# Order of evacuations in stage D, the form of stage A for one batch, and the place of one fold part, in an FFT and channel-mix kernel

## The chip, the cores and the metric

The kernel runs on one core of a Trainium2 chip. The metric is the device time of one execution in microseconds. TensorE multiplies matrices into PSUM, ScalarE and VectorE empty PSUM and compute elementwise, GpSimd and SyncE start DMAs. Each engine has its own instruction stream in program order; semaphores tie them together.

## The reference

```python
X = np.fft.fft(x, axis=1)            # x: 8 x 3072 x 256
X = np.fft.fft(X, axis=2)
x = X.real                           # input of the channel mix
x_prev = x shifted by one place along the sequence
xk = mu_k * x + (1 - mu_k) * x_prev
xr = mu_r * x + (1 - mu_r) * x_prev
k = np.maximum(xk @ w_k, 0.0)        # 256 -> 1024
v = k * k @ w_v                      # 1024 -> 256
r = 1.0 / (1.0 + np.exp(-(xr @ w_r)))
out = r * v                          # 8 x 3072 x 256, float32
```

## The kernel before, in words

The eight batches are computed one after the other, but in a software pipeline: while the channel mix of one batch runs, the Fourier transform of the next is made in between.

**Fourier transform of a batch.** *Fold* (VectorE): the sequence is added to its mirror image, in two parts h = 0 and 1. *quarters_1*, *quarters_2* (from batch 3 on; *butterfly* before that) make sums and differences over the feature axis on VectorE; quarters_2 is three instructions (L198, L200, L202) that write the tile eo. *Stage A* (TensorE): small matmuls of eo with tables, over the first factor of the sequence. *Stage D*: matmuls of stage A's result a with tables over the features, into g_all. *Stage C*: matmuls of g_all with the tables of the second factor, into pq. *halves*, *diff*, *mix* (VectorE) make the mixed inputs x of the channel mix.

**Channel mix.** The work is cut into 48 chunks of 512 places (8 batches, two mirror halves m, three parts each) and every chunk into four steps, so step 4n + ds is part ds of chunk n. In a step:

- a *k piece* (k_piece; matmuls L893, four of 512 columns) goes into a PSUM slot, and ScalarE's relu (L903) empties it; on every second step VectorE squares two pieces (L913);
- for each chunk an *r item* (L920, sigmoid L925), and the transform's items that are due ("x" items, added with at);
- a *v tile* (v_tile; L934, eight matmuls of 256 columns) of an earlier chunk, into half a bank, and after every second v tile an *output step* v_out: one VectorE instruction (L956) that multiplies and empties the bank, and two DMAs on SyncE's queue (L964);
- an *event*: a stage of the transform that works in two row groups of TensorE, rows 0 to 63 and 64 to 127 (matmuls L611 or L784). The steps listed in v_behind take their v tile out of the step and put it right behind the event before;
- the VectorE items that are due ("w" items). In the steps of OUT_FIRST the output step comes ahead of them, in others behind.

All of this order is written by hand as step numbers, and pin_order keeps it on every engine.

**PSUM.** Its eight banks are three double-bank slots, psW, handed out in turn by ps_w (k pieces, r items and the transform's stages take the next in the same ring), and two single banks, psV, handed out in turn by ps_v for the v tiles. v_bank gives a stage the psV bank that the next pair of v tiles will use: the *shared bank*. A slot or bank is written again only when everything that reads it is done. evac (L572, L574) is the evacuation; with "A" it is a ScalarE ACTIVATE.

**Stage A, two forms.** a_slot_0 computes slot 0 of the second part (two matmuls over 112 rows, L617) at an early step, with a small evacuation. a_all then computes all the rest in one event: three psW slots and the shared bank, pairs of matmuls of the two row groups side by side, and six evacuations of different sizes. For batch 2 these stand at steps 22 and 31.

**Stage D (d_all).** One event for the whole batch, at step s + 33 with s = 24t - 48, for batches t = 3 to 7: three psW slots and the shared bank; an evacuation of a slot is two ScalarE instructions. Behind it comes the v tile of step s + 34, then the k piece of s + 34 (into slot 0), the v tile of s + 35 (into the shared bank), the k pieces of s + 35 and s + 36 (slots 1 and 2), then an r item (slot 0 again).

**Around stage C of batch 2 (c_all, step 39).** It uses three slots and the shared bank, which the output step of step 38 empties. VectorE's order is: quarters_1 of batch 3 (step 36), quarters_2 (37), square (37), output step (38), fold of the second part (39), square (39).

Of the kernel before, what the change touches and what calls it, by code (L numbers as in the profile page):

```python
# [20 lines left out]
def _v(ap, extra_offset, free_dims):  # L21
    new_ap = [list(ap.ap[0])] + [[s, c] for (s, c) in free_dims]
    return dataclasses.replace(ap, offset=ap.offset + extra_offset, ap=new_ap)
# [16 lines left out]
def kernel(  # L40
# [10 lines left out]
    nc = tc.nc  # L51

    B, S, D = x.shape
    F = moe_w_k.shape[1]
    P = 128
    N1, R = 48, 64
    NSL = 27
    NU = 26
# [14 lines left out]
    def ps_slot(kind, n, cols):  # L73
        k = ps_n[kind] % n
        ps_n[kind] += 1
        return psum.tile([P, cols], FP32, name=f"ps{kind}{k}", tag=f"ps{kind}{k}", bufs=1)

    def ps_w():
        return ps_slot("W", 3, 1024)

    def ps_v():
        return ps_slot("V", 2, 512)
# [22 lines left out]
    xp_t, xm_t, p_t, eo_t = {}, {}, {}, {}  # L105
# [283 lines left out]
    w_h, w_h0 = w_hh[:, 0:WB], w_hh[:, WB:2 * WB]  # L389
# [176 lines left out]
    a_t = {}  # L566
# [3 lines left out]
    def evac(out_ap, in_ap, eng):  # L570
        if eng == "V":
            V.tensor_copy(out=out_ap, in_=in_ap)  # L572
        else:
            nc.scalar.activation(out=out_ap, in_=in_ap, func=AF.Copy)  # L574

    def a_tile(b):
        a_t[b] = y_pool.tile([P, 2, NU, 64], FP16, name="a")
# [23 lines left out]
    def v_bank():  # L601
        k = ps_n["V"] % 2
        return psum.tile([P, 512], FP32, name=f"psV{k}", tag=f"psV{k}", bufs=1)

    def side_by_side(lo, hi, n, f):
        for k in range(max(len(lo), len(hi))):
            if k == n:
                f()
            for items in (lo, hi):
                for out, w, r in items[k:k + 1]:  # L610
                    nc.tensor.matmul(out=out, lhsT=w, rhs=r, start=True, stop=True)  # L611
# [9 lines left out]
    def a_all(b):  # L621
# [13 lines left out]
        def out(ps, o, e, q, n, gs=(0, 1), step=512):  # L635
            evac(_v(a_t[b], 64 * NU * e + 16 * gs[0] + q, [(16, len(gs)), (32, WB), (1, n)]),
                 _v(ps, o, [(step, len(gs)), (1, WB), (WB, n)]), "A")
# [9 lines left out]
        out(ws[2], 0, 0, 9, 6)  # L647
        out(ws[2], 6 * WB, 1, 9, 3)

    def a_sum(b, h, i0, eng="A", m=4):  # L650


        if (h, i0) == (0, 0):
            a_tile(b)
        ps = ps_w() if m == 4 else ps_v()
        for i in range(m):
            parts = [(h, i0 + i + 1 - h, 0, 2 * WA, 0, 1)]
            if h and i0 + i == 7:
                parts = [(0, 0, 0, WA, WA, 1), (1, 7, 1, WA, 1, 2)]
            for half, q, o, n, w, step in parts:  # L660
                for k in range(2):
                    nc.tensor.matmul(out=_v(ps, 256 * i + o, [(2 * WA // n, n)]),  # L662
                                     lhsT=p_t[b, half][0:96, q, 128 * k:128 * k + 128],
                                     rhs=_v(w_pm[0:96], (WA + WB) * k + w,
                                            [(WA + WB, 2), (step, n // 2)]),
                                     start=(k == 0), stop=(k == 1))
        a_ps[b, h, i0] = ps
        if eng:
            a_evac(b, h, i0, eng, m)

    a_ps = {}

    def a_evac(b, h, i0, eng, m=4):
        evac(_v(a_t[b], 8 * h + i0, [(16, 2 * WA), (1, m)]),
             _v(a_ps[b, h, i0], 0, [(1, 2 * WA), (256, m)]), eng)
# [23 lines left out]
    def d_all(b):  # L699
        ws = [ps_w() for _ in range(3)]  # L700
        v = v_bank()

        def run(g, n):
            rows = (lo64, hi64)[g]
            ps, o, step = (ws[n], 512 * g, 256) if n < 3 else (v, 128 * g, 64)
            return [(ps[:, o + step * e + 64 * i:o + step * e + 64 * i + 64],
                     a_t[b][rows, e, 2 * u:2 * u + 2, :], w_d[rows, e])
                    for i, u in enumerate(range(4 * n, min(4 * n + 4, NU // 2))) for e in range(2)]

        def out(ps, n, k, gs=(0, 1), o=0, e=256):  # L710
            g, m = gs[0], len(gs)
            evac(_v(g_all, 1024 * n + g, [(1, m), (128, 2 * k), (2, 32)]),
                 _v(ps, o, [(512, m), (32, 2 * k), (1, 32)]), "A")
            evac(_v(g_all, 1024 * n + 64 + 128 * g, [(128, m), (256, k), (1, 64)]),
                 _v(ps, o + e, [(512, m), (64, k), (1, 64)]), "A")

        side_by_side(run(0, 3) + run(0, 0) + run(0, 1) + run(0, 2),
                     run(1, 0) + run(1, 1) + run(1, 2) + run(1, 3),
                     2, lambda: out(v, 3, 1, (0,), 0, 64))
        out(ws[0], 0, 4)  # L720
        out(ws[1], 1, 4)
        out(v, 3, 1, (1,), 128, 64)
        out(ws[2], 2, 4)

    def d_small(b, u, n, eng="A"):
# [214 lines left out]
    def v_part(c, ds, tbs):  # L940
        for tb in tbs:
            h = tb % 2
            if ds == 0 and h == 0:
                st["v", tb] = ps_v()
            for fc in (2 * ds, 2 * ds + 1):
                nc.tensor.matmul(out=st["v", tb - h][:, 256 * h:256 * h + 256],  # L946
                                 lhsT=k2_t[c][:, fc, 128 * tb:128 * tb + 128], rhs=wv_sb[:, fc],
                                 start=fc == 0 and h == 0, stop=fc == 7, skip_group_check=True)
# [31 lines left out]
    for a in range(2):  # L980
        nc.tensor.matmul(out=mu_ps[:, 2 * a:2 * a + 2], lhsT=mu_p[:, a], rhs=unit, start=True,
                         stop=True)
    for n in range(2):
        outer(mu_ps[:, 4 + n:5 + n], (tv(TO + n, 0, (1, P)), rv(ONE, 0, (1, 1))))
    keep_busy(NF[1], fill)
    a_sum(0, 0, 0)
    fold(0, 0, 5, 4)
    a_sum(0, 0, 4)
    nc.scalar.activation(out=muf_t, in_=mu_ps[:, 0:6], func=AF.Copy)
    loads()  # L990
    keep_busy(NF[2], ang_ps[1])
    fold(0, 1, 0, 4)
    a_sum(0, 1, 0, "A")
    fold(0, 1, 4, 4)
    fold(0, 0, 0, 1)
# [29 lines left out]
    for a in range(2):  # L1025
        t = x_t["t", a] = mix_pool.tile([P, 24, 64], FP16, name=f"t{a}")
# [25 lines left out]
    def at(step, f, *args):  # L1052
        work.setdefault((step, "x" if f in (a_item, a_sum, d_item, d_small, c_item, c_tiles, turned, minus_0, r_item, quarter_tables, a_slot_0) else "w"),
                        []).append((f, args))
# [5 lines left out]
    def event(step, *items):  # L1060
        work.setdefault((step, "e"), []).extend((f[0], f[1:]) for f in items)

    def v_behind(*steps):
        early_v.update(steps)
# [2 lines left out]
    nk = 4 * len(chunks)  # L1067

    LAG, EARLY, SHORT = 5, 3, 3
    OUT_FIRST = (12, 20, 28, 30, 36, 38, 40, *(24 * t - 48 + k for t in range(3, B) for k in (28, 32, 36)))  # L1070
    SQUARE_A = (6, 7, 8, 9)
    v_steps = {4 * n + tb + LAG: (c, tb) for n, c in enumerate(chunks) for tb in range(4)
               if n > EARLY or n == EARLY and tb >= 2}
# [59 lines left out]
    at(16, fold, 2, 0)  # L1133
    at(17, butterfly, 2, 0)
    event(18, (c_pairs, 1, 0, 8, "V"), (c_pairs, 1, 8, 8))
    event(20, (c_pairs, 1, 16, 8), (c_pairs, 1, 24, 4))
    v_behind(21)
    at(19, halves, 1, 0, 13)
    at(20, diff, 1, 0, 12)
# [13 lines left out]
    at(30, mix, 1, 1, 0, 1, 12, 24)  # L1153
    at(28, fold, 2, 1)
    at(29, butterfly, 2, 1)
    at(22, a_slot_0, 2)
    event(31, (a_all, 2))
    v_behind(32)
    at(28, r_item, (1, 0, 0))
    at(33, d_item, 2, 0)  # L1160
# [27 lines left out]
    for t in range(3, B):  # L1188
        s = 24 * t - 48

        def every(step, f, *args):
            at(s + step, f, t, *args)

        every(9, fold, 0)
        every(12, quarters_1, 0)
        every(13, quarters_2, 0)
        every(15, fold, 1)
        every(26, quarters_1, 1)
        every(27, quarters_2, 1)
        at(s + 18, a_slot_0, t)  # L1200
        event(s + 29, (a_all, t))
        event(s + 33, (d_all, t))
        at(s + 36, turned, 0, 13)
        event(s + 37, (c_all, t))
        v_behind(s + 30, s + 34, s + 35, s + 38)
        every(40, halves, 0, 15)
        every(42, halves, 15, 27)
        every(43, diff, 0, 26, (0,))
        every(44, diff, 0, 26, (1,))
        every(45, mix, 0, 0, 0)  # L1210
        every(46, mix, 0, 0, 1)
        every(48, mix, 1, 0, 0)
        every(49, mix, 1, 0, 1)
        every(52, mix, 0, 1, 0)
        every(54, mix, 0, 1, 1)
        every(58, mix, 1, 1, 0)
        every(59, mix, 1, 1, 1)
# [9 lines left out]
    for step in range(nk + LAG):  # L1227
# [3 lines left out]
        v = v_steps.get(step)  # L1231
# [5 lines left out]
        if step + 1 in early_v:  # L1237
            if step + 1 in v_steps:
                v_tile(*v_steps[step + 1])
            if step + 1 in p_steps:  # L1240
                v_part(*p_steps[step + 1])
        early = step in OUT_FIRST
        for v in o_steps.get(step, ()) if early else ():
# [40 lines left out]
```

## Time and profile before

| | |
|---|---|
| median of 3 runs | 429.43 us (429.33 to 429.53) |
| the profiled execution: its time, its span | 429.81 us, 428.0 us |
| busy: TensorE, VectorE, ScalarE | 420.0, 371.3, 334.0 us |
| granted TensorE clock | 1.0 throughout |
| DMA | 42.08 MB, mean 98 GB/s |

The span runs from the first to the last instruction. In a timeline row stand the start, the time taken, the engine, the line, the operation with its output and inputs, how many instructions were merged, and in brackets the idle time before with what ended it. Rows of TensorE's matmuls overlap: a matmul's row ends later than the next may start.

### The profile page before, as it was taken

The page shows a single profiled execution, that of the slowest core. Times are in us where ns is not written, and L with a number is a line of the kernel's source. Part 1 is how long each engine was busy: PE and PEld are TensorE (multiplying, and loading weights), DVE is VectorE, ACT ScalarE, POOL GpSimd, SP SyncE. Part 2 cuts the span into 40 slices and gives each one's busy share as a digit, 9 for nine tenths or more (in the row PEclk, how much of TensorE's full clock was granted, in tenths as well). Part 3 has the DMA queues.
Part 4 walks back from the last instruction along what each step waited for, and adds up shares of the span by engine and source line. Part 5 has one row for each costly group of instructions (what it writes and reads, how often), then busy time and mean ns, then how long its engine had stood idle before and what let it go on. Part 6 is the DMA issues. An engine that isn't in the chain of part 4 may idle for free.

```text
span 428.0 us, 9650 instructions
## 1 busy us (share of the span) xinstructions
PE 420.0 (98%) x3974; PEld 294.0 (69%) x3974; DVE 371.3 (87%) x593; ACT 334.0 (78%) x442; POOL 63.5 (15%) x99
## 2 busy tenths in 40 slices
PE   8999999999999999999999999999999999999996
PEld 3767766776767676776676667676677676766765
DVE  8899999999898899988999889988999776977643
ACT  7889887797769986699767997689866898666661
POOL 7378500200060001400032000500000000000000
PEclk9999999999999999999999999999999999999999
DMA  8779962632276222942249222772232232322333
GB/s 172 108 104 195 231 150 58 128 80 57 68 137 159 53 63 64 209 109 51 63 78 229 51 69 56 133 171 64 51 75 68 59 71 54 70 67 61 75 76 98
DMA packets 35104, 42.08 MB, mean 98 GB/s; under 512 B 4114, under 2 KB 31092, under 8 KB 35060
## 3 DMA queue, kind: packets, MB, share of 16 engines
q1 hardware_dynamic: 27488, 25.41, 24.2%
q0 software_dynamic: 7264, 15.80, 21.5%
q8 instruction: 31, 0.51, 0.5%
q10 hardware_dynamic: 308, 0.26, 0.2%
q14 instruction: 13, 0.11, 0.1%
HBM read 32.08 MB, written 25.17 MB: 134 GB/s over the span
## 4 chain that ended last, share of the span: by engine, by line
PE 79%; DVE 13%; ACT 5%; issue 2%; POOL 0%; DVEq 0%; POOLq 0%
PE psW L893 32%; PE psV L934 31%; PE psW L920 8%; ACT g_all L574 3%; DVE k L913 3%; DVE o L956 2%; PE psW L611 2%; DVE x L858 2%; DVE t L847 2%; ACT rl L903 1%; DVE p L172 1%; PE psW L235 1%; DVE eo L211 1%; PE psV L946 1%; PE psV L611 1%
## 5 line engine op out<-in xcount | busy, mean ns | idle before, releaser
L903 ACT ACTIVATE rl<-psW 128x1024 f16<-128x1024 f32 x192 | 194.9, 1034 | 80.2 <-PE psW L893 75.8
L893 PE MATMUL psW<-x,wk 128*128 128x512 f16 (+1 forms) x776 | 194.4, 377 | 0.6 <-ACT a L574 0.3
L934 PE MATMUL psV<-wv_sb,k 128*128 128x256 f16 x1424 | 184.2, 273 | 1.4 <-ACT g_all L574 1.4
L934 PEld LDWEIGHTS <-k 128*128 128x128 f16 x1424 | 136.6, 98 | 41.0 <-issue 2.8
L913 DVE TENSOR_TENSOR k<-rl 128x2048 f16<-128x2048 f16 (+1 forms) x100 | 115.6, 1156 | 34.0 <-ACT rl L903 33.9
L893 PEld LDWEIGHTS <-wk 128*128 128x128 f16 x776 | 75.7, 98 | 54.2 <-issue 0.9
L956 DVE SCALAR_TENSOR_TENSOR o<-psV,r 128x512 f32<-128x512 f32 (+1 forms) x97 | 65.8, 680 | 11.6 <-PE psV L934 11.2
L858 DVE TENSOR_TENSOR x<-y,t 128x1536 f16<-128x1536 f16 (+3 forms) x76 | 62.4, 827 | 2.2
L925 ACT ACTIVATE r<-psW 128x1024 f16<-128x1024 f32 x48 | 49.5, 1031 | 0.8 <-PE psW L920 0.8
L920 PE MATMUL psW<-wr,x 128*128 128x256 f16 x384 | 49.8, 273 | 0.0
L920 PEld LDWEIGHTS <-x 128*128 128x128 f16 x384 | 37.5, 98 | 14.1
L574 ACT ACTIVATE a<-psW 128x936 f16<-128x936 f32 (+4 forms) x37 | 29.8, 851 | 0.4 <-PE psW L662 0.4
L574 ACT ACTIVATE g_all<-psW 128x512 f16<-128x512 f32 (+5 forms) x47 | 26.3, 635 | 0.3 <-PE psW L684 0.2
L494 POOL IOTA gate<- 1x1 int32 x7 | 0.8, 121 | 165.8 <-DVE gate L493 165.8
L141 POOL DMA_INDIRECT xm<-in_x_dram,idx_g x18 | 22.8, 1265 | 5.5 <-issue 5.5
L172 DVE TENSOR_TENSOR p<-xp,xm 112x2304 f16<-112x2304 f16 (+6 forms) x19 | 21.7, 1143 | 0.4 <-issue 0.4
L847 DVE TENSOR_SCALAR t<-d,muf_t 128x1536 f16<-128x1536 f16 (+3 forms) x44 | 21.9, 508 | 0.1
L574 ACT ACTIVATE pq<-psW 128x1024 f16<-128x1024 f32 (+1 forms) x21 | 20.4, 1007 | 0.1
L847 DVE TENSOR_SCALAR t<-d,mu_m 128x1536 f16<-128x1536 f16 x32 | 19.8, 618 | 0.0
L835 DVE TENSOR_TENSOR d<-y 128x1664 f16<-128x1664 f16 (+5 forms) x19 | 16.7, 880 | 0.7 <-ACT y L574 0.6
L827 DVE TENSOR_TENSOR y<-pq 128x960 f16<-128x960 f16 (+3 forms) x28 | 15.7, 603 | 0.4
L946 PE MATMUL psV<-wv_sb,k 128*128 128x256 f16 x112 | 14.7, 273 | 0.0
(154 smaller groups left out, 238.2 us busy)
## 6 DMA issues: line engine op xcount, KB each, us to landing
out_dram<-o SPq DMA_DIRECT2D x189, 128.0 KB
xp<-in_x_dram POOLq DMA_DIRECT2D x12, 216.0 KB
xp<-in_x_dram POOLq DMA_DIRECT2D x13, 192.0 KB
xp<-in_x_dram POOLq DMA_DIRECT2D x2, 384.0 KB
wv_sb<-in_moe_w_v_dram POOLq DMA_DIRECT2D x1, 512.0 KB
xp<-in_x_dram SPq DMA_DIRECT2D x1, 480.0 KB
xp<-in_x_dram POOLq DMA_DIRECT2D x1, 432.0 KB
xm<-in_x_dram,idx_g POOLq DMA_INDIRECT x18
```

Of the source, the lines that this page charges most:

```text
L141: nc.gpsimd.indirect_dma_start(dst, None, src, bass.IndirectOffsetOnAxis(ap=idx, axis=0))
L172: V.tensor_tensor(out=p[:, q0:q0 + n], in0=xp[:, q0:q0 + n], in1=_v(xm, o + 256, [(-256, n), (-1, 256)]), op=ALU.add)
L574: nc.scalar.activation(out=out_ap, in_=in_ap, func=AF.Copy)
L847: V.tensor_scalar(out=dst, in0=src, scalar1=mu, scalar2=None, op0=ALU.mult)
L858: V.tensor_tensor(out=_v(x_t[b, j, m], o, [(64 * step, hi - lo), (step, 64)]), in0=y_t[b][:, lo + 3 * m:hi + 3 * m, a], in1=x_t["t", a][:, ...
L893: nc.tensor.matmul(out=st["k", ds][:, 512 * hs + lo:512 * hs + hi], lhsT=wk_sb[m][a][:, 128 * fc:128 * fc + 128], rhs=xk[:, a, 512 * i + l ...
L903: nc.scalar.activation(out=st["rl"][:, 2 * ds:2 * ds + 2], in_=st["k", ds].rearrange("p (f t) -> p f t", f=2), func=AF.Relu, bias=0.0, sca ...
L913: V.tensor_tensor(out=k2_t[c][:, lo:hi], in0=r, in1=r, op=ALU.mult)
L920: nc.tensor.matmul(out=ps[:, 256 * tb:256 * tb + 256], lhsT=x_t[b, 1, m][:, a, 512 * i + 128 * tb: 512 * i + 128 * tb + 128], rhs=wr_sb[m] ...
L925: nc.scalar.activation(out=st["r", c], in_=ps, func=AF.Sigmoid)
L934: nc.tensor.matmul(out=st["v", tb - h][:, 256 * h:256 * h + 256], lhsT=k2_t[c][:, fc, 128 * tb:128 * tb + 128], rhs=wv_sb[:, fc], start=(f ...
L956: V.scalar_tensor_tensor(out=o.rearrange("p a b -> p (a b)")[:, 0:256 * n], in0=st["v", t0][:, 0:256 * n], scalar=16.0, in1=st["r", c][:, ...
```

## The change

Three edits.

1. In d_all the second evacuation of the shared bank is put behind slot 0's and ahead of slot 1's.
2. Batch 2's stage A uses two functions that are new here, a_slots_0 and a_half. Its output goes into four double-bank slots, one for each part h and parity e, each evacuated by one ScalarE instruction of 832 elements per partition; the shared bank is not used. The half (h, e) = (0, 0) is made at step 20, behind two c_pairs events of batch 1; the others and the two matmuls of slot 0 at step 31. Step 30 leaves OUT_FIRST, so its output step comes behind that step's mix.
3. quarters_2 of batch 3's first part moves from step 37 to step 38, where the output step goes first.

```diff
+    def a_slots_0(b):
+        for e in range(2):
+            a_ps[b, 1, e] = ps_w()
+            nc.tensor.matmul(out=a_ps[b, 1, e][:, 2 * NU * 7:2 * NU * 8],
+                             lhsT=eo_t[b, 0][0:112, 0, e, :], rhs=w_h0, start=True, stop=True)
+
+    def a_half(b, h, e, eng="A"):
+        if (h, e) == (0, 0):
+            a_tile(b)
+        ps = a_ps[b, h, e] if h else ps_w()
+        for i in range(8):
+            for g in range(h and i == 7, 2):
+                rows = slice(64 * g, 64 * g + N1)
+                nc.tensor.matmul(out=_v(ps, 512 * g + 2 * NU * i, [(1, 2 * NU)]),
+                                 lhsT=eo_t[b, h][rows, i + 1 - h, e, :], rhs=w_h[rows],
+                                 start=True, stop=True)
+        evac(_v(a_t[b], 64 * NU * e + 8 * h, [(16, 2), (32, 2 * NU), (1, 8)]),
+             _v(ps, 0, [(512, 2), (1, 2 * NU), (2 * NU, 8)]), eng)
...
         out(ws[0], 0, 4)
+        out(v, 3, 1, (1,), 128, 64)
         out(ws[1], 1, 4)
-        out(v, 3, 1, (1,), 128, 64)
         out(ws[2], 2, 4)
...
-    OUT_FIRST = (12, 20, 28, 30, 36, 38, 40, *(24 * t - 48 + k for t in range(3, B) for k in (28, 32, 36)))
+    OUT_FIRST = (12, 20, 28, 36, 38, 40, *(24 * t - 48 + k for t in range(3, B) for k in (28, 32, 36)))
...
-    event(20, (c_pairs, 1, 16, 8), (c_pairs, 1, 24, 4))
+    event(20, (c_pairs, 1, 16, 8), (c_pairs, 1, 24, 4), (a_half, 2, 0, 0))
...
-    at(22, a_slot_0, 2)
-    event(31, (a_all, 2))
+    event(31, (a_slots_0, 2), (a_half, 2, 1, 0), (a_half, 2, 1, 1), (a_half, 2, 0, 1))
...
-        every(13, quarters_2, 0)
+        every(14 if t == 3 else 13, quarters_2, 0)
```

## The prediction

> **What bounds the kernel now.** I read the page's busy times first, then the list of what TensorE waited for, then the timeline around each of those waits.
>
> ```profile
> span 428.0 us, 9650 instructions
> PE 420.0 (98%) x3974; PEld 294.0 (69%) x3974; DVE 371.3 (87%) x593; ACT 334.0 (78%) x442; POOL 63.5 (15%) x99
> PE psV L934 <- ACT g_all L574: 1.4, 5, 0.3
> PE psV L611 <- DVE o L956: 0.4, 1, 0.4
> PE psW L893 <- ACT a L574: 0.3, 1, 0.3
> DVE k L913 <- ACT rl L903: 33.9, 32, 2.8
> ```
>
> TensorE is busy 98% of the span, and past its start-up only three waits are left in its list: five at L934 for ScalarE, one at L611 for VectorE, one at L893 for ScalarE. VectorE itself stands 33.9 us waiting for ScalarE's relus, so neither of the others is full. The change has one edit at each of the three places. A wait's idle column is not its price, because a matmul's row is longer than the time until the next may start. I price each wait by the distance between starts.
>
> **Stage D, five batches.** Batch 3 stands for all; TensorE first, then ScalarE, then the last of the five.
>
> ```profile
> 141.23 1.05 PE L934 MATMUL psV<-wv_sb,k 128*128 128x256 f16 x8
> 142.11 1.03 PE L893 MATMUL psW<-x,wk 128*128 128x512 f16 x4
> 143.43 1.03 PE L934 MATMUL psV<-wv_sb,k 128*128 128x256 f16 x8 [0.29 <-ACT g_all L574]
> 144.30 1.89 PE L893 MATMUL psW<-x,wk 128*128 128x512 f16 x8
> 146.02 1.04 PE L920 MATMUL psW<-wr,x 128*128 128x256 f16 x8
> ```
>
> ```profile
> 140.86 2.28 ACT L574 ACTIVATE g_all<-psW 128x512 f16<-128x512 f32 x4
> 142.98 0.40 ACT L574 ACTIVATE g_all<-psV 128x64 f16<-128x64 f32 x2
> 143.19 1.27 ACT L574 ACTIVATE g_all<-psW 128x512 f16<-128x512 f32 x2
> 144.24 3.06 ACT L903 ACTIVATE rl<-psW 128x1024 f16<-128x1024 f32 x3
> ```
>
> ```profile
> 344.13 1.03 PE L893 MATMUL psW<-x,wk 128*128 128x512 f16 x4
> 345.45 1.03 PE L934 MATMUL psV<-wv_sb,k 128*128 128x256 f16 x8 [0.29 <-ACT g_all L574]
> ```
>
> A group of work unhindered takes 0.87 us from start to start (141.23 to 142.11, 143.43 to 144.30). After the k piece at 142.11 the v tile should start at 142.98. It starts at 143.43, which is 0.05 after the evacuation of the shared bank ends (142.98 + 0.40 = 143.38). The loss is 1.32 - 0.87 = 0.45 us, and in the last batch 345.45 - 344.13 = 1.32 gives the same. Five times 0.45 is 2.25 us, where the idle column has 1.4.
>
> The edit removes and adds no instruction. It moves two small evacuations past two large ones. ScalarE issues four large ones from 140.86 to 142.98, so 1.06 for a slot, and the two small ones in 0.21 (142.98 to 143.19). The shared bank is then free at about 140.86 + 1.06 + 0.40 = 142.32, 0.66 before the v tile's own time of 142.98. The wait goes whole.
>
> What is late next? Slot 1 comes free 0.21 later. Its evacuations end about 143.15 now, so 143.36; the k piece that takes it now starts at 144.30, then at 143.85: 0.49 spare. Slot 2 is out at 143.19 + 1.27 = 144.46 in both orders; its k piece moves from 145.17 to 144.72: 0.21 spare after the 0.05 of the signal. The r item at 146.02 moves to 145.57; it takes the slot that the first relu reads, which starts at 144.24 as before and ends about 145.37: 0.15 spare. Those are the thinnest. The second and third relu move up with TensorE, since the k pieces that they read end earlier. So I count 2.25. If ScalarE ran 0.2 later than worked out, 0.05 to 0.2 a batch would come back.
>
> **Batch 2's stage A.** First the step where the first half is put (TensorE, then ScalarE), then the step with the wait, then the evacuations by form.
>
> ```profile
> 59.83 1.04 PE L934 MATMUL psV<-wv_sb,k 128*128 128x256 f16 x8
> 60.80 0.52 PE L784 MATMUL psW<-m_cs,g_all 64*128 64x64 f16 x24
> 61.25 1.05 PE L934 MATMUL psV<-wv_sb,k 128*128 128x256 f16 x8
> 62.13 1.03 PE L893 MATMUL psW<-x,wk 128*128 128x512 f16 x4
> 64.73 0.22 PE L617 MATMUL psW<-w_hh,eo 112*128 112x52 f16 x2
> ```
>
> ```profile
> 59.16 1.94 ACT L903 ACTIVATE rl<-psW 128x1024 f16<-128x1024 f32 x2 [0.48 <-PE psW L893]
> 61.24 1.51 ACT L574 ACTIVATE pq<-psW 128x1024 f16<-128x1024 f32 x2
> ```
>
> ```profile
> 82.17 1.04 PE L934 MATMUL psV<-wv_sb,k 128*128 128x256 f16 x8
> 83.31 0.20 PE L611 MATMUL psW<-w_hh,eo 48*128 48x52 f16 x1
> 84.25 1.05 PE L934 MATMUL psV<-wv_sb,k 128*128 128x256 f16 x8
> 86.00 1.04 PE L920 MATMUL psW<-wr,x 128*128 128x256 f16 x8
> 87.36 1.02 PE L893 MATMUL psW<-x,wk 128*128 128x512 f16 x4 [0.33 <-ACT a L574]
> ```
>
> ```profile
> 82.37 1.02 ACT L903 ACTIVATE rl<-psW 128x1024 f16<-128x1024 f32 x1 [0.71 <-PE psW L893]
> 85.95 1.36 ACT L574 ACTIVATE a<-psW 128x624 f16<-128x624 f32 x2
> ```
>
> ```profile
> L574 ACT ACTIVATE a<-psW 128x936 f16<-128x936 f32 x12 | 11.8, 1046 | 0.0
> L574 ACT ACTIVATE a<-psW 128x832 f16<-128x832 f32 x7 | 6.0, 866 | 0.4 <-PE psW L662 0.4
> ```
>
> Two losses stand at step 31. Two-row-group matmuls follow a v tile after 0.97 (59.83 to 60.80), so stage A should start at 83.14 and starts at 83.31: 0.17 lost, because its shared bank waits for the output step of step 30. And the k piece at 87.36 should start at 86.00 + 0.87 = 86.87: 0.49 lost, because its slot is out only at 85.95 + 1.36 = 87.31. Together 0.66.
>
> The other form has the same 64 matmuls. TensorE's price of a pair: (84.25 - 83.31) for 31 pairs against (61.25 - 60.80) for 12 gives 0.026 us each. The first half adds 8 pairs, 0.21, at step 20, behind c_pairs, which already works in two row groups. Its two matmuls of L617 (0.06) move from step 22 to 31. Step 31 keeps 24 rounds instead of 31; in two of them the upper rows work alone, since their partners are the two of L617. The net is 32 rounds for 31, 0.03.
>
> Its waits: at step 20 the half takes the slot that the relu of step 20 reads, out at 59.16 + 1.94 = 61.10; TensorE gets there at about 61.16. The next k piece, 62.13 + 0.21 = 62.34, takes the slot of the first pq evacuation, out at about 61.24 + 1.02 = 62.26. Both fit by 0.03 or so; I charge 0.02 for them. The half's evacuation stands on ScalarE from about 62.7 (the pq pair ends at 61.24 + 1.51 = 62.75) to 63.7, ahead of one relu. The k piece that takes its slot comes two groups after the one at 62.34, at 64.1.
>
> No row shows this evacuation's shape. The 832-element rows say 0.87 us, but they read one run of places; the 936-element ones read and write two places as this does and say 1.05. I take 0.95, nearest to the second, scaled by size. At step 31 the halves start at 83.35, three evacuations issue from 83.78 at about 0.86, and the last ends at 86.5. TensorE wants its slot at 87.36 - 0.66 + 0.03 = 86.73. At 1.05 each the last would end at about 86.75 and 0.1 us would be lost; at 0.87 there is 0.4 to spare. The whole is 0.66 - 0.03 - 0.02, about 0.6 us.
>
> The output step of step 30 goes behind two mix instructions and is 0.9 us later, its two output DMAs on SP with it. Its bank is then next wanted by a v tile of step 33, after 88, and not by stage A, so I cost it at nothing. If stage A still used that bank it would cost 0.9.
>
> **Batch 3's first fold part.** VectorE, TensorE and ScalarE before stage C of batch 2.
>
> ```profile
> 98.97 0.76 DVE L198 TENSOR_TENSOR eo<-t 112x1152 f16<-112x1152 f16 x1
> 100.54 1.22 DVE L913 TENSOR_TENSOR k<-rl 128x2048 f16<-128x2048 f16 x1
> 101.67 0.68 DVE L956 SCALAR_TENSOR_TENSOR o<-psV,r 128x512 f32<-128x512 f32 x1
> ```
>
> ```profile
> 99.26 1.04 PE L934 MATMUL psV<-wv_sb,k 128*128 128x256 f16 x8
> 100.99 1.04 PE L934 MATMUL psV<-wv_sb,k 128*128 128x256 f16 x8
> 102.41 0.19 PE L611 MATMUL psV<-m_cs,g_all 64*128 64x64 f16 x1 [0.38 <-DVE o L956]
> ```
>
> ```profile
> 97.69 1.02 ACT L903 ACTIVATE rl<-psW 128x1024 f16<-128x1024 f32 x1 [0.51 <-PE psW L733]
> ```
>
> Stage C should start at 100.99 + 0.97 = 101.96 and starts at 102.41: 0.45 lost. Its bank is emptied by the output step at 101.67, behind quarters_2 (three instructions, 98.97 to 100.54, 1.57 us) and a square. With quarters_2 behind it, the square can start at 98.97 (its relu is done at 98.71), and the output step when its v tile is done, 99.26 + 1.04 = 100.30. It ends at 101.0, well ahead. The 1.57 us then stand in front of the next fold and square. Since the output step leaves 101.67 - 100.30 = 1.37 earlier, these come only 0.2 later than now. TensorE's list has no wait for a square past the start-up, and this one is needed by a v tile two steps on, so I cost the 0.2 at nothing; with that cover gone it would be 0.2. Gain 0.45.
>
> **The sum.** 2.25 + 0.6 + 0.45 = 3.3 us. The profiled execution took 429.81 us around a span of 428.0; it would take 426.5. The median shown is 0.38 lower, 429.43, and I forecast its counterpart, 426.1.
>
> The trace has TensorE starting a k piece's four 512-column matmuls every 0.87 us, without a gap, from 60 us on but for these waits. The Trainium skill, "Perfetto Trace Analysis", section "Identifying the Most-Contended Engine", says that matmul busy time is a poor measure and the share of weight loads a better one. The page of the profile has 69% there. By that rule TensorE has headroom and could make up a lost 0.45 elsewhere, and the sum would be near zero, not 3.3. This trace speaks against it, since each group after a wait keeps its 0.87.
>
> **The rivals.** (1) *ScalarE takes the place of the bank in stage D.* The eight evacuations and the relus behind them keep their total, and the r item has 0.15 spare. If half of each 0.45 returns there, 1.1 us is lost: 427.2. For it: the thin margins. Against it: relus two and three start when their k pieces end. (2) *One of the two small edits gives nothing*, by a new wait at steps 20 to 22 or at the halves' evacuation: 0.45 to 0.65 less, 426.6 to 426.8. (3) *TensorE is not the bound*, and the saved waits reappear as waits for VectorE or ScalarE: 429.4. VectorE's 33.9 us of waiting speak against it. (4) *Slower: the v tile's release is counted on all of stage D's evacuations*, not on the shared bank's own. Then each v tile would wait for slot 2, 144.46 + 0.05 instead of 143.43, 1.08 worse five times: 429.43 + 5.4 - 1.05 = 433.8. It decides as soon as the release is later than 143.43. Against it: today TensorE starts 0.05 after the bank's own evacuation and 1.03 before slot 2's.
>
> **Chances.** Forecast 0.74, (1) 0.10, (2) 0.09, (3) 0.04, (4) 0.03. The forecast's own range is 425.8 to 426.5. The range 425.7 to 427.0 holds it, the second rival and part of the first, and the evacuation's both ends. A measurement of this kernel can tell about 0.2%, 0.86 us, from no change. Faster by more: 0.93; within: 0.04; slower by more: 0.03.
>
> **What would show it.** After: no row "PE psV L934 <- ACT g_all L574"; in stage D of each batch a v tile 0.87 after its k piece; the small psV evacuations directly behind slot 0's pair; stage C of batch 2 0.97 after its v tile; the k piece of step 33 0.87 after its r item; 16 matmuls of L611's kind at about 61 us. TensorE's end moves by 3.3. I am wrong if new rows of TensorE waits appear at k pieces or r items behind stage D, or at 61 to 64 us, or if TensorE's waits vanish and the span does not follow.

## The result and the profile after

The changed kernel takes 426.07 us (median of 6 runs, 425.98 to 426.54) against 429.38 us of the kernel before in the same comparison. The ratio is 0.9923, with a 95% interval of 0.9910 to 0.9936. The forecast was 426.1. The profiled execution took 426.17 us; the first lines of its page:

```profile
span 424.4 us, 9646 instructions
PE 418.4 (99%) x3974; PEld 294.1 (69%) x3974; DVE 371.3 (87%) x593; ACT 332.4 (78%) x438; POOL 64.2 (15%) x99
PE 98%; DVE 1%; issue 0%; POOL 0%; ACT 0%; POOLq 0%
```

The third line is the chain that ended last: 98% of it is now TensorE. Before, VectorE and ScalarE had 18% of it:

```profile
PE 79%; DVE 13%; ACT 5%; issue 2%; POOL 0%; DVEq 0%; POOLq 0%
```

TensorE has the same 3974 matmuls, ScalarE four instructions less. Stage A's old form has eight evacuations: six behind a_all's matmuls, as counted above, one in between them, and slot 0's. The new form has four. The complete list of what TensorE waited for is now this:

```profile
PE psW L235 <- DVE xm L266: 1.0, 1, 1.0
PE psW L912 <- DVE x L1049: 0.3, 1, 0.3
PE psW L378 <- DVE rw L308: 0.2, 1, 0.2
PE psV L378 <- DVE rw L308: 0.2, 1, 0.2
```

All four belong to the first 19 us. The three waits that the change was aimed at are gone, and none took their place. (The new functions shift line numbers: the k piece is L912 here, the v tile L953, the r item L939, the output step L975, stage A's halves L663, slot 0's matmuls L653.)

**Stage D**, batch 3, TensorE and then ScalarE:

```profile
140.53 1.03 PE L912 MATMUL psW<-x,wk 128*128 128x512 f16 x4
141.40 1.04 PE L953 MATMUL psV<-wv_sb,k 128*128 128x256 f16 x8
142.27 1.89 PE L912 MATMUL psW<-x,wk 128*128 128x512 f16 x8
144.00 1.04 PE L939 MATMUL psW<-wr,x 128*128 128x256 f16 x8
```

```profile
139.28 1.19 ACT L574 ACTIVATE g_all<-psW 128x512 f16<-128x512 f32 x2
140.35 0.35 ACT L574 ACTIVATE g_all<-psV 128x64 f16<-128x64 f32 x2
140.56 2.31 ACT L574 ACTIVATE g_all<-psW 128x512 f16<-128x512 f32 x4
```

The shared bank is empty at 140.70, before the v tile comes at 141.40. That is 0.87 after its k piece; it was 1.32.

**Batch 2's stage A**, the halves on TensorE and their evacuations on ScalarE:

```profile
60.34 0.52 PE L803 MATMUL psW<-m_cs,g_all 64*128 64x64 f16 x24
60.71 0.37 PE L663 MATMUL psW<-w_hh,eo 48*128 48x52 f16 x16
61.01 1.05 PE L953 MATMUL psV<-wv_sb,k 128*128 128x256 f16 x8
...
81.87 1.04 PE L953 MATMUL psV<-wv_sb,k 128*128 128x256 f16 x8
82.75 0.22 PE L653 MATMUL psW<-w_hh,eo 112*128 112x52 f16 x2
83.60 1.05 PE L953 MATMUL psV<-wv_sb,k 128*128 128x256 f16 x8
85.35 1.04 PE L939 MATMUL psW<-wr,x 128*128 128x256 f16 x8
86.22 1.03 PE L912 MATMUL psW<-x,wk 128*128 128x512 f16 x4
```

```profile
62.19 0.87 ACT L574 ACTIVATE a<-psW 128x832 f16<-128x832 f32 x1
83.31 2.38 ACT L574 ACTIVATE a<-psW 128x832 f16<-128x832 f32 x3 [0.21 <-PE psW L663]
```

The k piece of step 33 starts 0.87 after its r item (86.22 - 85.35); it was 1.36. Its slot is empty at 83.31 + 2.38 = 85.69, half a microsecond early.

**Before stage C of batch 2**, VectorE and TensorE:

```profile
97.89 1.22 DVE L932 TENSOR_TENSOR k<-rl 128x2048 f16<-128x2048 f16 x1
99.19 0.69 DVE L975 SCALAR_TENSOR_TENSOR o<-psV,r 128x512 f32<-128x512 f32 x1
99.80 0.75 DVE L198 TENSOR_TENSOR eo<-t 112x1152 f16<-112x1152 f16 x1
```

```profile
99.86 1.04 PE L953 MATMUL psV<-wv_sb,k 128*128 128x256 f16 x8
100.83 0.20 PE L611 MATMUL psV<-m_cs,g_all 64*128 64x64 f16 x1
```

The output step ends at 99.88, and stage C starts 0.97 after its v tile; it was 1.42. quarters_2 now stands behind the output step.

**Where the spans differ.** The two profiled spans differ by 3.6 us, more than the medians (3.31). The first matmul of stage C of batch 1 and the last group of matmuls show why. First the kernel before, then after:

```profile
56.64 0.64 PE L784 MATMUL psW<-m_cs,g_all 64*128 64x64 f16 x32
422.76 1.38 PE L934 MATMUL psV<-wv_sb,k 128*128 128x256 f16 x10
```

```profile
56.19 0.64 PE L803 MATMUL psW<-m_cs,g_all 64*128 64x64 f16 x32
418.76 1.60 PE L953 MATMUL psV<-wv_sb,k 128*128 128x256 f16 x12
```

At the first, before anything that the change touches, the second execution is already 0.45 ahead. From there to the last matmul's end it is 424.14 - 56.64 = 367.50 before and 420.36 - 56.19 = 364.17 after: 3.33. The start of an execution varies, the rest hardly does, so I compare stretches that begin at this matmul.

### The profile page after: what moved, and what is told of

The parts are those of the page before. It is cut to its first block, busy times and chain, and to the rows that moved or that the text cites. A ratio compares the mean times of both kernels' runs of the same rounds, so it can differ in the third digit from the quotient of the medians.

```text
span 424.4 us, 9646 instructions
## 1 busy us (share of the span) xinstructions
PE 418.4 (99%) x3974; PEld 294.1 (69%) x3974; DVE 371.3 (87%) x593; ACT 332.4 (78%) x438; POOL 64.2 (15%) x99
## 4 chain that ended last, share of the span: by engine, by line
PE 98%; DVE 1%; issue 0%; POOL 0%; ACT 0%; POOLq 0%
PE psW L912 39%; PE psV L953 37%; PE psW L939 10%; PE psV L965 3%; PE psW L611 3%; PE psW L235 1%; PE psV L611 1%; PE psW L681 1%; PE psW L703 1%; PE psV L378 1%; PE psW L771 0%; PE psW L803 0%; DVE rw L308 0%; PE psV L703 0%; PE psW L663 0%
## 5 line engine op out<-in xcount | busy, mean ns | idle before, releaser
L912 PE MATMUL psW<-x,wk 128*128 128x512 f16 (+1 forms) x776 | 194.4, 377 | 0.3 <-DVE x L1049 0.3
L953 PE MATMUL psV<-wv_sb,k 128*128 128x256 f16 x1424 | 184.2, 273 | 0.0
L953 PEld LDWEIGHTS <-k 128*128 128x128 f16 x1424 | 136.8, 98 | 38.9
L912 PEld LDWEIGHTS <-wk 128*128 128x128 f16 x776 | 75.7, 98 | 53.7 <-issue 0.4
L975 DVE SCALAR_TENSOR_TENSOR o<-psV,r 128x512 f32<-128x512 f32 (+1 forms) x97 | 65.7, 680 | 10.0 <-PE psV L953 9.0
L939 PE MATMUL psW<-wr,x 128*128 128x256 f16 x384 | 49.8, 273 | 0.0
L939 PEld LDWEIGHTS <-x 128*128 128x128 f16 x384 | 37.5, 98 | 14.1
L574 ACT ACTIVATE a<-psW 128x832 f16<-128x832 f32 (+4 forms) x36 | 29.0, 851 | 0.2 <-PE psW L663 0.2
```

Source lines behind the costliest of these rows:

```text
L912: nc.tensor.matmul(out=st["k", ds][:, 512 * hs + lo:512 * hs + hi], lhsT=wk_sb[m][a][:, 128 * fc:128 * fc + 128], rhs=xk[:, a, 512 * i + l ...
L939: nc.tensor.matmul(out=ps[:, 256 * tb:256 * tb + 256], lhsT=x_t[b, 1, m][:, a, 512 * i + 128 * tb: 512 * i + 128 * tb + 128], rhs=wr_sb[m] ...
L975: V.scalar_tensor_tensor(out=o.rearrange("p a b -> p (a b)")[:, 0:256 * n], in0=st["v", t0][:, 0:256 * n], scalar=16.0, in1=st["r", c][:, ...
```

## The experiments

The theory was the prediction's: TensorE's issue is the bound, each edit removes one kind of wait, and what is removed comes off the time. The main rivals were that TensorE has room, that releases are counted on a whole stage, and that the gains come back elsewhere. The table has every run. The columns are stretches of each trace. The first three marks are first matmuls: of stage C of batch 1 (C1, step 18), stage C of batch 2 (C2) and stage D of batch 3 (D3). D7 is the last matmul of stage D of batch 7, and the end is the start of the kernel's last matmul. Then comes the ratio to the kernel before with its interval.

| kernel | C1 to C2 | C2 to D3 | D3 to D7 | D7 to end | ratio (95%) |
|---|---|---|---|---|---|
| before | 45.77 | 37.96 | 202.76 | 80.74 | |
| after | 44.63 | 37.96 | 201.01 | 80.29 | 0.9923 (0.9910 to 0.9936) |
| d_only | 45.76 | 37.94 | 200.99 | 80.30 | 0.9959 (0.9945 to 0.9973) |
| a_only | 45.27 | 37.95 | 202.76 | 80.73 | 0.9991 (0.9982 to 1.0) |
| f_only | 45.33 | 37.96 | 202.76 | 80.74 | 0.9991 (0.9982 to 1.0) |
| a_f | 44.63 | 37.96 | 202.74 | 80.74 | 0.9968 (0.9957 to 0.9980) |
| d_first | 45.78 | 37.96 | 203.77 | 81.00 | 1.0033 (1.0021 to 1.0045) |
| d_last | 45.68 | 37.95 | 207.03 | 81.82 | 1.0124 (1.0109 to 1.0140) |
| drop30 | 46.68 | 37.95 | 202.75 | 80.75 | 1.0020 (1.0010 to 1.0030) |
| keep30 | 44.63 | 37.96 | 201.00 | 80.30 | 0.9923 (0.9908 to 0.9939) |
| pe_more | 44.63 | 37.97 | 202.51 | 80.95 | 0.9977 (0.9967 to 0.9988) |
| act_more | 44.63 | 37.96 | 200.99 | 80.30 | 0.9927 (0.9914 to 0.9941) |
| c_swap | 44.63 | 37.94 | 201.01 | 80.30 | 0.9922 (0.9908 to 0.9935) |
| c_swap45 | 44.63 | 37.83 | 200.98 | 80.30 | 0.9914 (0.9899 to 0.9929) |

Where a kernel does the same, a stretch repeats within 0.1 us and mostly within 0.02. That is far finer than the medians.

### The edits one by one

**d_only** (before, with stage D's order alone):

```diff
         out(ws[0], 0, 4)
+        out(v, 3, 1, (1,), 128, 64)
         out(ws[1], 1, 4)
-        out(v, 3, 1, (1,), 128, 64)
```

> Stage D's order alone. Theory (each edit removes its own TensorE wait, and the gains add): five waits of 0.45 us go, 2.25 in all, so about 427.15 against 429.4; the two other waits of before stay in TensorE's list. Rival (the gain comes out of the three edits together, or from the start of the run, which is 0.46 us earlier in the profile of after): less than 1.5 us, 427.9 or more.

427.68 us against 429.72. The last two stretches hold the waits behind the five stages D, four and one. They are 1.77 and 0.44 shorter, 2.21 together, or 0.44 a batch. The other two waits are still in its list, unchanged. The edit works alone and by the amount expected.

**a_only** (after, with stage D's order and quarters_2 as before):

```diff
-        out(v, 3, 1, (1,), 128, 64)
         out(ws[1], 1, 4)
+        out(v, 3, 1, (1,), 128, 64)
...
-        every(14 if t == 3 else 13, quarters_2, 0)
+        every(13, quarters_2, 0)
```

> Batch 2's stage A in the other form alone, with step 30 out of OUT_FIRST. Theory: the 0.17 before stage A and the 0.49 of the k piece of step 33 go, less 0.03 to 0.05 for one more round of matmuls: 0.6 to 0.7 us, about 428.75. The stage D rows in TensorE's list stay as they are. Rival (the halves' evacuations or step 20 bring a new wait): under 0.3 us.

429.31 us against 429.72, with an interval of the ratio that reaches 1.0; the first stretch, which is the finer measure, is 0.50 shorter. That is less than the theory's 0.6 to 0.7 and more than the rival's 0.3. TensorE and VectorE before stage C of batch 2 in this kernel:

```profile
100.20 1.04 PE L953 MATMUL psV<-wv_sb,k 128*128 128x256 f16 x8
101.81 0.19 PE L611 MATMUL psV<-m_cs,g_all 64*128 64x64 f16 x1 [0.57 <-DVE o L975]
```

```profile
99.93 1.22 DVE L932 TENSOR_TENSOR k<-rl 128x2048 f16<-128x2048 f16 x1
101.07 0.68 DVE L975 SCALAR_TENSOR_TENSOR o<-psV,r 128x512 f32<-128x512 f32 x1
```

Stage C should start at 100.20 + 0.97 = 101.17 and starts at 101.81: it loses 0.64, where before it lost 0.45. TensorE arrives 0.69 earlier, but VectorE's output step, still behind quarters_2 and a square, came only 0.5 earlier. So 0.2 us of the gain is given back one stage later.

**f_only** (before, with quarters_2 of batch 3 one step later):

```diff
-        every(13, quarters_2, 0)
+        every(14 if t == 3 else 13, quarters_2, 0)
```

> quarters_2 of batch 3 one step later alone. Theory: the 0.45 us before stage C of batch 2 goes, 428.95. Rival (VectorE gives it back at the next square): no gain, 429.4.

429.36 us against 429.72, again with an interval that reaches 1.0; the first stretch is 0.44 shorter, and the next is unchanged at 37.96. The gain is what was expected, and VectorE does not give it back.

**a_f** (after, with stage D's order as before). If the reading of a_only is right, the two edits together must bring more than their sum.

```diff
-        out(v, 3, 1, (1,), 128, 64)
         out(ws[1], 1, 4)
+        out(v, 3, 1, (1,), 128, 64)
```

> Stage A's form and the later quarters_2 together, stage D's order as before. Alone they took 0.50 and 0.44 us out of the stretch from stage C of batch 1 to the first matmul of stage C of batch 2 (45.77 before, 45.27 and 45.33). Theory (stage A's gain was 0.7 and 0.2 of it came back as a longer wait for VectorE's output step ahead of stage C, which the later quarters_2 takes away): the pair gives more than the sum, 1.14, so that stretch is 44.63 and the time about 1.1 below before. Rival (the gains just add): 44.83.

The first stretch is 44.63, so 1.14 shorter, against 0.94 for the sum. The time is 428.30 against 429.35. The third edit is worth 0.44 alone and 0.64 behind the second.

### The place of the shared bank's evacuation

**d_first** (before, with that evacuation ahead of slot 0's):

```diff
+        out(v, 3, 1, (1,), 128, 64)
         out(ws[0], 0, 4)
         out(ws[1], 1, 4)
-        out(v, 3, 1, (1,), 128, 64)
```

> The shared bank's second evacuation ahead of slot 0's instead of behind it, nothing else changed from before. Theory: the v tile waits no more (2.25 gained), but slot 0 is out 0.21 later, and its k piece has no time to spare (slot 0 ends at 142.05, the k piece starts at 142.11): about 0.2 lost five times, so 428.15 to 428.3, with five new waits of a k piece for ScalarE. Rival (releases are counted on the whole stage's evacuations): like the order of after, 427.15, or no change.

Slower than before, 430.90 against 429.72. The mechanism that was expected is there, five new waits of a k piece, but its size was not. TensorE and ScalarE:

```profile
140.74 1.05 PE L934 MATMUL psV<-wv_sb,k 128*128 128x256 f16 x8
142.32 1.02 PE L893 MATMUL psW<-x,wk 128*128 128x512 f16 x4 [0.53 <-ACT g_all L574]
```

```profile
140.14 0.34 ACT L574 ACTIVATE g_all<-psV 128x64 f16<-128x64 f32 x2
140.85 0.34 ACT L574 ACTIVATE g_all<-psV 128x64 f16<-128x64 f32 x2 [0.37 <-PE psV L611]
141.08 3.36 ACT L574 ACTIVATE g_all<-psW 128x512 f16<-128x512 f32 x6
```

The second small pair waits 0.37 for matmuls. The upper rows' part of the shared bank is the last that stage D computes, so ScalarE stands idle in front of slot 0. Slot 0's evacuation starts 0.94 after the first small pair, and the k piece is 1.58 behind its v tile instead of 0.88: 0.70 lost against 0.45 gained, five times 0.25 the wrong way. My expectation had counted the 0.21 that the pair takes and not what it waits for.

**d_last** (before, with that evacuation behind slot 2's):

```diff
         out(ws[1], 1, 4)
-        out(v, 3, 1, (1,), 128, 64)
         out(ws[2], 2, 4)
+        out(v, 3, 1, (1,), 128, 64)
```

> The shared bank's second evacuation behind slot 2's, nothing else changed from before. Theory: the v tile starts 0.05 after that evacuation ends, about 144.51 instead of 143.43, so 1.08 more in each of five batches, 5.4 in all: 434.8. Rival (TensorE has room and makes up what it loses): about 429.4.

434.75 us against 429.43, and 434.8 was expected. TensorE and ScalarE:

```profile
141.58 1.03 PE L893 MATMUL psW<-x,wk 128*128 128x512 f16 x4
143.96 1.03 PE L934 MATMUL psV<-wv_sb,k 128*128 128x256 f16 x8 [1.35 <-ACT g_all L574]
```

```profile
143.50 0.40 ACT L574 ACTIVATE g_all<-psV 128x64 f16<-128x64 f32 x2
```

The v tile follows the end of the pair (143.90) by 0.06. It is 2.38 behind its k piece instead of 1.32. The four places in the order now have their prices: first 430.9, behind slot 0 427.7, behind slot 1 429.4 to 429.7, last 434.8.

### The output step of step 30

**drop30** (before, with the output step behind the mix) and **keep30** (after, with it ahead of the mix):

```diff
-    OUT_FIRST = (12, 20, 28, 30, 36, 38, 40,
+    OUT_FIRST = (12, 20, 28, 36, 38, 40,
```

> Before, with step 30 taken out of OUT_FIRST and nothing else. Stage A of batch 2 still uses the shared bank, which that output step empties. Theory: the output step is 0.9 us later, and stage A's first matmul with it, so 430.3. Rival (the output step's place does not matter): 429.4.

> After, with step 30 back in OUT_FIRST. Theory: stage A no longer uses the bank that this output step empties, so the place costs and brings nothing: 426.1 within 0.1. Rival (the mix must go first to gain): 426.4 or more.

drop30 takes 430.42 against 429.43, and its first stretch is 0.91 longer. TensorE and VectorE there:

```profile
81.88 1.04 PE L934 MATMUL psV<-wv_sb,k 128*128 128x256 f16 x8
83.93 0.18 PE L611 MATMUL psV<-w_hh,eo 48*128 48x52 f16 x1 [1.02 <-DVE o L956]
```

```profile
83.19 0.68 DVE L956 SCALAR_TENSOR_TENSOR o<-psV,r 128x512 f32<-128x512 f32 x1
```

Stage A in the old form waits for the bank that this output step empties. keep30's median of 426.43 lies outside the expected 426.1 within 0.1, and by itself it would speak for the rival. The stretches decide: they are after's to 0.01 us, and keep30 reaches stage C of batch 1 at 56.39 us, 0.20 later than after, before anything in which the two differ. Its ratio to the kernel before is after's too. So in the new form the place of that step is worth nothing, and the prediction's zero for this edit holds, with its reason.

### Is TensorE the bound?

**pe_more** (after, with 20 more matmuls of 256 columns) and **act_more** (after, with 20 more small ScalarE copies):

```diff
+        if tb == 0 and c in chunks[24:44]:
+            nc.tensor.matmul(out=st["v", tb][:, 0:256], lhsT=k2_t[c][:, 0, 0:128],
+                             rhs=wv_sb[:, 0], start=True, stop=True)
```

```diff
+    def idle_copy():
+        nc.scalar.activation(out=warm, in_=zeros[:, 0:1], func=AF.Copy)
+
+    for n in range(24, 44):
+        at(4 * n + 2, idle_copy)
```

> After, with 20 more matmuls of 256 columns, one ahead of the first v tile in each of 20 chunks (it writes what the next one overwrites). Theory: TensorE's issue is the bound, so each costs its 0.107 us, 2.1 in all: 428.2. Rival (the weight loads' 69% means that TensorE has room): 426.1.

> After, with 20 more small ScalarE copies of one column (about 0.2 us each), one in each of 20 chunks, away from the transform's stages. Theory: ScalarE has idle time there and nothing waits for it: 426.1. Rival (ScalarE's total sets the time): 430.

pe_more takes 428.33, and its last two stretches are 1.50 and 0.66 longer than after's: 2.16 for 20 matmuls, 0.108 each, nothing hidden. act_more takes 425.95 and has after's stretches, though its 20 copies take 0.19 to 0.49 us each in the trace, 5.1 together. So TensorE's issue is the bound in the steps where these matmuls and copies stand (the last two stretches), and these copies are free there. Larger additions to ScalarE's work were not run.

### A version beyond both

After's list of waits has nothing left behind the first 19 us, but the k piece of step 41 comes 1.01 behind its r item:

```profile
103.50 1.04 PE L939 MATMUL psW<-wr,x 128*128 128x256 f16 x8
104.51 1.02 PE L912 MATMUL psW<-x,wk 128*128 128x512 f16 x4
```

**c_swap** swaps two evacuations of batch 2's stage C:

```diff
         out(1)
+        if b == 2:
+            out(2)
         evac(_v(pq, 128 * 24, [(256, 2), (1, 128)]), _v(v, 0, [(256, 2), (1, 128)]), "A")
-        out(2)
+        if b != 2:
+            out(2)
```

> After, with one thing more: in batch 2's stage C the shared bank's last evacuation goes behind slot 2's. In after's trace the k piece of step 41 starts at 104.51, 0.05 after slot 2's evacuation ends, 0.14 later than the r item before it allows; the shared bank is wanted by a v tile only at 105.37. Theory: 0.14 us gained, 425.9, and that k piece 0.87 to 0.98 behind its r item. Rival (the shared bank becomes the wait, as it was in stage D): slower by up to 0.1.

The expected 0.14 us did not come: the median is 426.11, and the stretch C2 to D3 is 37.94 against after's 37.96. TensorE and VectorE in c_swap (L915 is the k piece, L942 the r item, L956 the v tile):

```profile
103.39 1.04 PE L942 MATMUL psW<-wr,x 128*128 128x256 f16 x8
104.27 1.03 PE L915 MATMUL psW<-x,wk 128*128 128x512 f16 x4
...
116.53 1.04 PE L956 MATMUL psV<-wv_sb,k 128*128 128x256 f16 x8
117.41 1.14 PE L915 MATMUL psW<-x,wk 128*128 128x512 f16 x4
118.39 1.04 PE L942 MATMUL psW<-wr,x 128*128 128x256 f16 x8
```

```profile
116.73 0.96 DVE L880 TENSOR_TENSOR x<-y,t 128x1536 f16<-128x1536 f16 x1
```

The k piece at 104.27 follows at once, 0.88, so the 0.13 is won. It is lost again at 117.41: this group takes 1.14 instead of 1.03, because its second matmul starts only behind the half of x that VectorE ends at 117.69. The mixes stand back to back on VectorE behind a square that waits for ScalarE's relu, and the swap does not bring that relu forward. **c_swap45** also puts that mix one step earlier:

```diff
-    at(46, mix, 2, 0, 0, 1)
+    at(45, mix, 2, 0, 0, 1)
```

> The kernel with stage C's two last evacuations swapped for batch 2, and the last mix of batch 2 (2, 0, 0, 1) at step 45 instead of 46, ahead of a square. Without that the k piece of step 48 gave back 0.12 of the 0.14 won, waiting for that mix. Theory: the mix ends 1.1 us earlier, that wait goes, and from stage C of batch 2 to stage D of batch 3 it takes 37.82 instead of 37.96; the time is about 0.13 below after's, which a median hardly shows. Rival (the square behind it becomes the wait): 37.9 or more.

The stretch C2 to D3 is 37.83 and the time 425.89, the ratio 0.9914 (0.9899 to 0.9929). The trace shows 0.13 us less than after there; the medians alone could not.

## Why the prediction was right

**The sum.** Forecast 3.3 us, measured 3.31 by the medians and 3.33 from stage C of batch 1 to the last matmul. The likeliest case came true, at 426.07 for 426.1.

**Stage D, forecast 2.25.** Measured 2.20 in after and 2.21 in d_only, from the last two stretches. The step that mattered was to price the wait by starts (1.32 - 0.87) and not by the idle column, which had 1.4 for the five and would have given under two thirds.

**Batch 2's stage A, forecast about 0.6.** Measured 0.69 up to the k piece of step 33 (87.36 to 86.22, less the 0.45 of the start). Here small terms were mis-sized, by about 0.09 together. The evacuation, taken at 0.95 and bounded by 0.87 and 1.05, takes 0.87, so the lower row was the right one although it reads one run of places; it set only the margin. The 0.02 for waits at step 20 did not arise: the halves start at once behind c_pairs. And the extra round cost nothing. From the v tile ahead of the stage to the one behind it, the new form takes 83.60 - 81.87 = 1.73, and the half at step 20 adds 61.01 - 60.34 - 0.45 = 0.22: 1.95. The old form takes 0.97 + 0.94 without its wait, and 0.06 for slot 0 at step 22: 1.97.

**The first fold part, forecast 0.45.** f_only gives 0.44. But the forecast added it to the others as if they were independent, and they are not: a_only shows that 0.2 of stage A's gain would have stayed in front of stage C. The sum came out right because both edits are in, which the forecast did not argue.

**What is late next.** The forecast named the r item and slot 2's k piece, with 0.15 and 0.21 to spare. Neither waits in after. The list missed the thinnest place: in the trace of before, slot 0's evacuation ends at 142.05 and its k piece starts at 142.11, with nothing to spare. The edit leaves that order alone; d_first shows the price of changing it.

**A gap that the forecast did not see.** It said that from 60 us on TensorE has no gap but the waits that it priced. In before the k piece of step 41 already starts 1.00 behind its r item (105.08 to 106.08), 0.13 late, and is in no list of waits. The edits do not touch it, so the sum does not suffer; c_swap and c_swap45 found and removed it.

**The rivals.** ScalarE in place of the bank (427.2): no such row. Nothing gained by a small edit: each of the two gives 0.44 or more. TensorE not the bound: pe_more speaks against it with 0.108 us for each matmul added. The Trainium skill, "Perfetto Trace Analysis", section "Identifying the Most-Contended Engine", judges TensorE's headroom by two measures, MFU (the share of peak FLOP/s) and the busy share of weight loads. Here the second is 69%, yet pe_more finds no headroom in its steps, and the measurement decides; MFU was not worked out. Releases counted on the whole stage: in after the v tile starts at 141.40, while the stage's last evacuations run until 140.56 + 2.31 = 142.87. d_last cannot tell, since there the shared bank's evacuation is the stage's last.

## What to carry to other kernels

Price a wait on a pipelined engine from start to start, against the same pair of groups where nothing waits. Before an evacuation is moved, look at both ends of it: when its slot is wanted, and when its data is ready. Where waits follow each other, a gain at the first can lengthen the next, so test edits alone and in pairs, and compare stretches of the trace rather than whole times when less than one per cent is at stake.

## What the runs showed of the hardware

The time to the first matmul of stage C of batch 1 scatters between 56.09 us (act_more, c_swap) and 56.92 us (d_only) over the fourteen profiled executions, whose edits all stand behind it; in the other stretches the same program repeats mostly within 0.02 us. ScalarE's evacuation of 832 elements out of two banks takes 0.87 us, while that of 936 took 1.05 with a like pattern, written in runs of nine elements where the new form has eight. By its share of elements the smaller would take 0.93; why it takes less is not shown.
